# Result buffers of their own with whole-row transfers, and a tile of y moved behind the last products

## The chip, the cores and the metric

The kernel runs on one core of a Trainium2 chip. The metric is the device time of one execution in microseconds (us). The matrix engine is called TensorE (PE in the profile, PEld for its weight loads), the others are VectorE (DVE), ScalarE (ACT), GpSimd (POOL) and SyncE (SP). SP, ACT and POOL issue transfers.

## What is computed

The input x has 2048 rows of 512. With xn its layer norm without scale, the kernel computes a Fourier mixing s of xn and a gate g, and adds:

```python
xn  = layernorm(x)                                   # over the 512 columns
a   = xn @ dft_hid_re.T ;  b = xn @ dft_hid_im.T
s   = dft_seq_re @ a - dft_seq_im @ b                # 2048 x 512
h   = relu(xn @ w1 + b1)                             # 2048 x 1792
g   = silu((h * h) @ w2 + b2)                        # 2048 x 512
out = x + s * g
```

## The kernel before, in words

All products are float32 values split into a high and a low part (fp32r); each product takes three passes (high-high, high-low, low-high). Larger products go by a scheme of seven half-size products in place of eight (Strassen's), so their operands need sums of quarters (`sums_a`, `sums_b`), a rounding to the high part on ScalarE (L68) and a subtraction for the low part on VectorE (L71), and seven accumulators are joined at the end (`combine`: a copy on ScalarE, L260, then four steps on VectorE, L261 to L264).

**First stage.** The sequence transform is done first: for each block c of 256 columns of the transform (c = 0 to 7), over eight chunks j of 256 rows. Blocks 0 and 1 are done plainly, blocks 2 to 7 by the seven products. A chunk of the transform is loaded (`load_c`, L210), summed and split (`moving`) two chunks ahead; three raw loads are in flight. TensorE takes 42 matmuls a chunk (L321). Behind the last chunk the accumulators are combined and split into `pq`. The second factor, the hidden transform, is `stage2(c, t)`: 25 matmuls (L308) into one accumulator, a copy to the buffer `ysb` (L313) and a store of 128 rows of y (L315). The two tiles t = 0 and 1 of block c - 1 are done behind chunks 1 and 2 of block c. In this stage a scheduler sets the order on each engine, from the order in which the code is written.

In block 7 the next stage is prepared too: the rows of mean and scale (`load_rows`), two halves of the transposed input (`xt_half`: a load, two steps L346, sums, split), and the loads of the prepared first weights (`load_w1`, L501), which take the places of chunks of xn as TensorE is done with them.

**Last stage.** The order on each engine is written out by hand. First the hidden layer: 28 units, `hidden(n, c, p)`, for four blocks c of 512 rows and seven pairs p of hidden tiles (L572), each combined, squared and stored. Unit 0 comes first, then the two tiles of y of block 7, then the other units. Then the outer product: the same 28 units, `outer` (L620), whose operands are fetched, summed and split two units ahead (`operand`, L597, L228 to L230, L68, L71). After the seventh unit of a block the seven accumulators are combined into `e`, a buffer of four 128 x 512 results, C21, C11, C22 and C12, named z in the profile. There is one place for `e`; each block uses it again. `finish(*done, h)` runs behind the units p = 1 and p = 2 of the following block (p = 1 and 4 in the last): it takes silu on ScalarE (L656), multiplies by y (`fin`, L660) in place, and GpSimd adds the result into `out` in DRAM, where x was copied earlier (L650). The last block's results are handled in a tail of their own, in which x is loaded (`load_fin`) and added on VectorE.

Transfers on one engine's queue are issued in the order of the program; an instruction that waits holds up those behind it.

Of the kernel before, what the change touches and what calls it, by code (L numbers as in the profile page):

```python
# [10 lines left out]
ALU = mybir.AluOpType  # L11

P = 128
S, D, F = 2048, 512, 1792
NS, ND, NF = S // P, D // P, F // P
NJ, NP = NS // 2, NF // 2
# [45 lines left out]
def fnet_gated_kernel(ctx, tc, x, xt, ct, wd, w1, w2, b1, b2, out):  # L62
# [28 lines left out]
    def buf(tag, shape, name, dtype=F32, bufs=1):  # L91
        return pool.tile(shape, dtype, tag=tag, bufs=bufs, name=name)
# [539 lines left out]
    def load_fin(c):  # L632

        fin[c] = []
        for n, src in enumerate((Y[c], x[c * TC:(c + 1) * TC])[:1 + (c == NTC - 1)]):
            for m in range(2):
                tag = f"pq{n}{m}" if c < NTC - 1 else (("g0a", "sx"), ("g0b", "pq10"))[n][m]
                t = buf(tag, [P, 2, 512], f"fin{c}_{n}{m}")
                for i in range(2):
                    nc.sync.dma_start(t[:, i].rearrange("p (k e) -> p k e", k=2), at(src, 2 * m + i))  # L640
                fin[c].append(t)

    def finish(c, e, h):

        for k in (2, 0) if h == 0 else (1, 3):
            silu(e, k)
            times(c, e, k)
        for k in range(2):
            n = c * TC + (1 - h) * 256 + k * P
            nc.gpsimd.dma_start(out[n:n + P].rearrange("p (b e) -> p b e", b=2), e[:, h:4:2, k * 256:(k + 1) * 256],  # L650
                                accum_op=ALU.add)

    def silu(e, k, cols=slice(0, 2)):

# [3 lines left out]
    def times(c, e, k, cols=slice(0, 2)):  # L658
        w = slice(cols.start * 256, cols.stop * 256)
        nc.vector.tensor_tensor(e[:, k, w], e[:, k, w], fin[c][k // 2][:, k % 2, w], op=ALU.mult)  # L660
# [22 lines left out]
    for c, j in steps:  # L683
        if j == 0:
            ms = banks(c)
        g = part.pop((c, j))
        for p in ORDER:
            a, (grp, b) = PRODUCTS[p]
            mm(product(ms, p), XC[j][:, a], lambda b_: g[grp][:, b_, b], j == 0, j == NJ - 1)
        if c == PLAIN:  # L690
            if j == 4:
                nc.vector.transpose(stats_t, stats.rearrange("p m h j -> p (m h j)"))
                for q in range(4):
                    nc.sync.dma_start(rows[:, q * 32:(q + 1) * 32], stats_t[q * 32:(q + 1) * 32, :])
        if j in (1, 2):
            y_stored = stage2(c - 1, j - 1)
        if PLAIN <= c < PLAIN + NTC - 1 and j == 2:
            part_ = slice((c - PLAIN) * TC, (c - PLAIN + 1) * TC)
            with tc.issue_after(y_stored.ins):
                nc.sync.dma_start(out[part_], x[part_])  # L700
        if (c, j) in jobs:
            make_w(*jobs[c, j])
        if j == NJ - 1:
            e = buf("e", [P, 4, 512], f"c{c}")
            combine(e, ms)
            for m, dh, k in ((0, 0, C11), (1, 1, C22), (1, 0, C12), (0, 1, C21)):
                pq(c, m, dh, e[:, k])
        prep()
        if c == NC - 1:

            if j == 2:
                e = buf("e", [P, 8, 256], "rows0")
                load_rows(0, e[:, 0:4])
            if j in (2, 4):
                first = xt_half(0, j // 2 - 1, lambda k: e[:, 4:8] if (j, k) == (2, "r") else
                                turn_of(k, True))
                next(first)
            if j in (3, 6):
                list(first)
                kept.clear()  # L720
            if j > 3:
                load_w1(j - 4)

# [243 lines left out]
```

## Time and profile before

| | |
|---|---|
| median of 3 runs | 700.67 us (700.66 to 702.34) |
| the profiled execution | 700.18 us, span from first to last instruction 698.4 us |
| TensorE busy | 682.2 us, 98% of the span |
| VectorE / ScalarE / GpSimd busy | 578.7 / 346.0 / 15.6 us |
| granted TensorE clock, mean | 0.997 |

A line of a group or timeline names the source line, the engine, the operation and "written <- read". In square brackets or behind the bar stands the idle time of the engine before it and what ended that. In windows the five busy times are those of PE, PEld, DVE, ACT and POOL, followed by the granted clock, the DMA engines' share and GB/s. For transfers the last number is the time from issue to landing.

### The profile page before, as it was taken

How to read it: one execution, taken by the hardware profiler on the slowest of the kernel's cores; microseconds unless marked ns; L12 is line 12 of the kernel's file. 1: busy time of each engine (PE TensorE's matmuls, PEld its weight loads, DVE VectorE, ACT ScalarE, POOL GpSimd, SP SyncE). 2: the span in 40 equal slices, each digit the busy share in tenths (PEclk: the TensorE clock that was granted, in tenths of full speed). 3: DMA queues.
4: the chain of work that ended last, by engine and by line, in shares of the span. 5: the costliest groups of instructions: out<-in, count | busy, mean ns of one | idle time of the engine just before them, and what ended most of it. 6: DMA issues, size and time to landing. Idle time of an engine off the chain costs nothing.

```text
span 698.4 us, 12740 instructions
## 1 busy us (share of the span) xinstructions
PE 682.2 (98%) x5179; PEld 645.3 (92%) x5179; DVE 578.7 (83%) x866; ACT 346.0 (50%) x463; POOL 15.6 (2%) x20
## 2 busy tenths in 40 slices
PE   8999999999999999999999999999999999989797
PEld 5778889999999999999999989999999999979797
DVE  7998975589599698797798697989988799969696
ACT  3444644334353544544452326675867864435351
POOL 0000000000000000000000000000000100101011
PEclk9999999999999999999999999999999999999999
DMA  8622440733674763845835998284487954656655
GB/s 321 237 91 92 139 171 27 252 138 134 216 268 136 271 226 111 302 132 173 298 93 189 400 381 265 117 297 170 166 294 313 367 203 161 156 168 153 180 168 104
DMA packets 52250, 141.09 MB, mean 202 GB/s; under 512 B 4912, under 2 KB 18736, under 8 KB 50992
## 3 DMA queue, kind: packets, MB, share of 16 engines
q1 hardware_dynamic: 44896, 122.46, 50.2%
q10 hardware_dynamic: 3456, 12.58, 4.5%
q0 software_dynamic: 3840, 5.24, 4.2%
q8 instruction: 40, 0.66, 0.4%
q14 instruction: 18, 0.15, 0.1%
HBM read 97.00 MB, written 46.42 MB: 205 GB/s over the span
## 4 chain that ended last, share of the span: by engine, by line
PE 75%; DVE 14%; DMA 4%; issue 4%; ACT 2%; POOL 0%; DVEq 0%; ACTq 0%; POOLq 0%; SPq 0%
PE m_b L321 21%; PE yps L308 13%; PE hps L572 9%; PE pq_b L374 7%; PE hps_b L572 5%; DVE block L71 4%; PE m_bb L321 4%; PE m_ba L321 4%; PE m L620 3%; PE hps_ba L572 3%; DMA out<-z 2%; PE pq_ba L374 2%; DMA raws<-in_xt 1%; PE pq_bb L374 1%; PE hps_bb L572 1%
## 5 line engine op out<-in xcount | busy, mean ns | idle before, releaser
L321 PE MATMUL m_b<-g,block 128*128 128x256 f32 x1080 | 129.0, 276 | 0.0
L321 PEld LDWEIGHTS m_b<-g,block 128*128 128x128 f32 x1080 | 125.5, 188 | 0.1
L68 ACT ACTIVATE g<-raws 128x768 fp32r<-128x768 f32 (+2 forms) x65 | 57.4, 885 | 88.7 <-PE m_b L321 41.1
L71 DVE TENSOR_TENSOR g<-raws,g 128x768 fp32r<-128x768 f32 (+2 forms) x65 | 65.5, 1008 | 40.1 <-ACT g L68 40.0
L308 PE MATMUL yps<-wd,pq 128*128 128x512 f32 (+1 forms) x414 | 92.8, 374 | 0.0
L308 PEld LDWEIGHTS yps<-wd,pq 128*128 128x128 f32 x414 | 74.4, 188 | 13.7
L71 DVE TENSOR_TENSOR g<-sums,g 128x1024 fp32r<-128x1024 f32 x48 | 58.7, 1222 | 12.3 <-ACT g L68 12.3
L572 PE MATMUL hps<-xT,block 128*128 128x256 f32 x504 | 59.1, 276 | 0.0
L68 ACT ACTIVATE g<-sums 128x1024 fp32r<-128x1024 f32 x48 | 50.3, 1049 | 16.7 <-PE m_ba L321 7.8
L572 PEld LDWEIGHTS hps<-xT,block 128*128 128x128 f32 x504 | 58.0, 188 | 0.0
L374 PE MATMUL pq_b<-g,block 128*128 128x512 f32 x180 | 47.4, 394 | 0.5 <-DVE g L71 0.4
L321 PE MATMUL m_b<-g,xc 128*128 128x256 f32 x360 | 45.0, 276 | 0.0
L321 PEld LDWEIGHTS m_b<-g,xc 128*128 128x128 f32 x360 | 42.8, 188 | 0.1
L620 PE MATMUL m_b_o<-w,block 128*128 128x256 f32 x360 | 42.6, 276 | 0.0
L374 PEld LDWEIGHTS pq_b<-g,block 128*128 128x128 f32 x180 | 33.2, 188 | 9.6 <-DVE block L71 2.1
L620 PEld LDWEIGHTS m_b_o<-w,block 128*128 128x128 f32 x360 | 41.6, 188 | 0.0
L572 PE MATMUL hps_b<-xT,block 128*128 128x256 f32 x288 | 34.9, 276 | 0.3 <-DVE xT L71 0.3
L68 ACT ACTIVATE block<-hr 128x1792 fp32r<-128x1792 f32 (+1 forms) x15 | 23.8, 1587 | 21.8 <-PE m_bb_o L620 6.1
L222 DVE TENSOR_TENSOR sums<-raws 128x512 f32<-128x512 f32 x49 | 33.6, 686 | 1.0 <-DMA raws<-in_ct 0.7
L572 PEld LDWEIGHTS hps_b<-xT,block 128*128 128x128 f32 x288 | 33.6, 188 | 0.5 <-DVE xT L71 0.5
L583 ACT ACTIVATE raws<-raws,b1s 128x512 f32<-128x512 f32 x42 | 28.0, 716 | 12.2 <-DVE raws L263 12.0
L620 PE MATMUL m_b_o<-block 128*128 128x256 f32 x270 | 32.1, 276 | 0.0
(236 smaller groups left out, 1210.1 us busy)
## 6 DMA issues: line engine op xcount, KB each, us to landing
raws<-in_ct SPq DMA_DIRECT2D x63, 512.0 KB, 3.6
w1d<-w0g SPq DMA_DIRECT2D x21, 512.0 KB, 3.2
block<-w1d SPq DMA_DIRECT2D x6, 1792.0 KB, 10.4
hd<-raws ACTq DMA_DIRECT2D x18, 512.0 KB, 4.9
hr<-hd SPq DMA_DIRECT2D x15, 512.0 KB, 4.4
block<-w2d SPq DMA_DIRECT2D x3, 1792.0 KB, 14.2
y<-ysb SPq DMA_DIRECT2D x16, 256.0 KB, 3.3
fin<-y SPq DMA_DIRECT2D x16, 256.0 KB, 5.3
```

The lines of the kernel that those rows point to most:

```text
L68: nc.scalar.activation(hi, src, AF.Copy)
L71: return nc.vector.tensor_tensor(lo, src, hi.bitcast(F32), op=ALU.subtract)
L222: nc.vector.tensor_tensor(t[:, 0:2], r[:, 0:1].to_broadcast([P, 2, 256]), r[:, 1:3], op=ALU.add)
L308: nc.tensor.matmul(ps[:, s], PQ[c, m, k // 2][:, a_, w:w + P], WD[m, k][:, b_, s], start=n == 0, stop=n > len(todo) - 3, skip_group_check= ...
L321: nc.tensor.matmul(ps[:, d * CW:(d + 1) * CW], w[:, a_, d * P:(d + 1) * P], mv(b_), start=first and d == 0 and (a_, b_) == (HI, HI), stop= ...
L374: nc.tensor.matmul(accs[c][k], w, g[:, b_, 2 * h:2 * h + 2], start=j == 0 and h == 0 and (a_, b_) == (HI, HI), stop=j == NJ - 1 and h == 1 ...
L572: nc.tensor.matmul(product(ms, k), W1[p][a][:, a_, q * P:(q + 1) * P], xT[c, q][:, b_, b], start=share not in first, stop=q == 1 and (a_, ...
L583: nc.scalar.activation(x_[:, s], x_[:, s], AF.Relu, bias=b1s[:, f:f + 1])
L620: nc.tensor.matmul(m[:, k * 256:(k + 1) * 256], g[:, a_, a, k * P:(k + 1) * P], W2[p][b][:, b_], start=p == 0 and k == 0 and (a_, b_) == ( ...
```

## The change

```diff
@@ load_fin
-                tag = f"pq{n}{m}" if c < NTC - 1 else (("g0a", "sx"), ("g0b", "pq10"))[n][m]
+                tag = f"pq{n}{m}" if c < NTC - 1 else (("g0a", "sx"), ("g0b", "xc0"))[n][m]
@@ finish
-        for k in (2, 0) if h == 0 else (1, 3):
+        z = buf(f"pq1{h}", [P, 2, 2, 256], f"z{c}_{h}")
+        for b, k in enumerate((C11, C12) if h == 0 else (C21, C22)):
             silu(e, k)
-            times(c, e, k)
-        for k in range(2):
-            n = c * TC + (1 - h) * 256 + k * P
-            nc.gpsimd.dma_start(out[n:n + P].rearrange("p (b e) -> p b e", b=2), e[:, h:4:2, k * 256:(k + 1) * 256],
-                                accum_op=ALU.add)
+            nc.vector.tensor_tensor(z[:, :, b], e[:, k].rearrange("p (k e) -> p k e", k=2),
+                                    fin[c][k // 2][:, k % 2].rearrange("p (k e) -> p k e", k=2), op=ALU.mult)
+        n = c * TC + h * 256
+        nc.gpsimd.dma_start(out[n:n + 256].rearrange("(k p) e -> p k e", k=2), z.rearrange("p k b e -> p k (b e)"),
+                            accum_op=ALU.add)
@@ the chunks of the first stage
-        if j in (1, 2):
-            y_stored = stage2(c - 1, j - 1)
+        if j in ((1, NJ - 1) if c == NC - 1 else (1, 2)):
+            y_stored = stage2(c - 1, int(j > 1))
@@ the same, in block 7
+            if j in (3, 5):
+                list(first)
+                kept.clear()
             if j == 2:
                 e = buf("e", [P, 8, 256], "rows0")
                 load_rows(0, e[:, 0:4])
-            if j in (2, 4):
-                first = xt_half(0, j // 2 - 1, lambda k: e[:, 4:8] if (j, k) == (2, "r") else
+            if j in (2, 3):
+                first = xt_half(0, j - 2, lambda k: e[:, 4:8] if (j, k) == (2, "r") else
                                 turn_of(k, True))
                 next(first)
-            if j in (3, 6):
-                list(first)
-                kept.clear()
```

In `finish` the product with y is written to one of two buffers, z0 and z1 (places pq10 and pq11), as 256 whole rows of 512; each half of a block goes out in one transfer of 512 KB with rows of 2 KB, where it went in two of 256 KB with pieces of 1 KB. The two upper quarters come first, then the two lower. Since pq10 is taken, the last block's second half of x lands in xc0, the place of the first pair of second weights.

In block 7 the second tile of y of block 6 is made behind chunk 7 and no longer behind chunk 2. The second half of the transposed input is requested behind chunk 3 (before: 4) and worked on behind chunk 5 (before: 6).

The scheduler makes of this the following. On TensorE in block 7 (`m_...` are the accumulators of the block, `g_7_j` the split chunk j, `yps_1` the tile of y that moves, `hps` the first unit of the next stage), before:

```order
L321 MATMUL m_ba_3648<-g_7_2_3694,block 128x256 x6
L308 MATMUL yps_1_3827<-wd_676,pq_0_0_3624 128x512 x6
L308 MATMUL yps_1_3827<-wd_676,pq_0_1_3633 128x512 x6
L308 MATMUL yps_1_3827<-wd_753,pq_1_0_3630 128x512 x6
L308 MATMUL yps_1_3827<-wd_753,pq_1_1_3627 128x512 x5
L308 MATMUL yps_1_3827<-wd_753,pq_1_1_3627 128x256 x2
L321 MATMUL m_bb_3649<-g_7_3_3776,block 128x256 x6
```

The tile stands between chunks 2 and 3. In the change its first seven matmuls stand within chunk 6,

```order
L321 MATMUL m_b_7_3646<-g_7_6_3948,block 128x256 x6
L321 MATMUL m_b_7_3646<-g_7_6_3949,block 128x256
L321 MATMUL m_b_7_3647<-g_7_6_3949,block 128x256
L321 MATMUL m_ba_3648<-g_7_6_3949,block 128x256
L308 MATMUL yps_1_4105<-wd_676,pq_0_0_3624 128x512 x6
L308 MATMUL yps_1_4105<-wd_676,pq_0_1_3633 128x512
L321 MATMUL m_bb_3649<-g_7_7_4000,block 128x256
L321 MATMUL m_b_7_3646<-g_7_6_3949,block 128x256 x5
```

and the other 18 between the last product of chunk 7 and the first unit of the hidden layer:

```order
L321 MATMUL m_ba_3648<-g_7_7_4001,block 128x256 x6
L308 MATMUL yps_1_4105<-wd_676,pq_0_1_3633 128x512 x5
L308 MATMUL yps_1_4105<-wd_753,pq_1_0_3630 128x512 x6
L308 MATMUL yps_1_4105<-wd_753,pq_1_1_3627 128x512 x5
L308 MATMUL yps_1_4105<-wd_753,pq_1_1_3627 128x256 x2
L572 MATMUL hps_bb<-xT_0_3900,block 128x256 x3
```

So the products of chunks 3 to 7 move forward by the tile, and the tile moves back to the stage's end. On SP's queue in the same block (`raws<-in_ct` the last load of the transform, `block<-w1d` prepared weights, `y_69<-ysb` stores of y):

```order
 L210 DMA raws<-in_ct 128x1024
 L315 DMA y_69<-ysb_3772 128x512
+L501 DMA block<-w1d_903 128x3584
 L210 DMA raws<-in_ct 128x1024
-L501 DMA block<-w1d_903 128x3584
-L315 DMA y_69<-ysb_3772 128x512
 L501 DMA block<-w1d_904 128x3584
 L340 DMA raws<-in_xt 128x1024
```

```order
 L506 DMA w1a_4209<-w1d_909 128x2x768
 L507 DMA w1b_4210<-w1d_909 128x2x1024
+L315 DMA y_69<-ysb_3772 128x512
 L315 DMA y_69<-ysb_4254 128x512 x2
 L333 DMA rows_4295<-rows 128x256 x4
```

The first weight passes the load of chunk 7, and the second store of y goes behind all seven weights, right ahead of the two stores of the next block. On ScalarE at the end of the second block of 512 rows in the last stage (`z_6618` is the buffer of the combination, `m_..._o` the accumulators), with the semaphores that each instruction waits for, before:

```order
L68 ACTIVATE block<-raws 128x1792 [waits DVE_49,DMAHW1_49,PE_49,Activation_49]
L260 ACTIVATE z_6618<-m_bc_o_6260 128x512 [waits DMASW6_49,DMASW5_49,DMASW7_49,DMASW4_49,PE_49]
L613 ACTIVATE m_ba_o_6628<-b2s 128x512
L613 ACTIVATE m_b_o_6629<-b2s 128x512 [waits DVE_49]
L613 ACTIVATE m_b_o_6630<-b2s 128x512 [waits DVE_49,PE_49]
```

and in the change:

```order
L68 ACTIVATE block<-raws 128x1792 [waits DVE_49,DMAHW1_49,PE_49,Activation_49]
L260 ACTIVATE z_6618<-m_bc_o_6260 128x512 [waits PE_49]
L613 ACTIVATE m_ba_o_6628<-b2s 128x512
L613 ACTIVATE m_b_o_6629<-b2s 128x512 [waits DVE_49]
L613 ACTIVATE m_b_o_6630<-b2s 128x512 [waits DVE_49,PE_49]
```

The order is the same; the four waits for GpSimd's transfers (DMASW) are gone from L260. GpSimd's queue holds six transfers from z where it held twelve.

## Prediction

> **What bounds the kernel now.** I read the page's engine shares first, then who TensorE waited for over the whole span, then the windows and the timeline at those waits.
>
> ```profile
> PE 682.2 (98%) x5179; PEld 645.3 (92%) x5179; DVE 578.7 (83%) x866; ACT 346.0 (50%) x463; POOL 15.6 (2%) x20
> PE m L620 <- DVE z L261: 3.5, 1, 3.5
> PE m_bc_o L620 <- ACT z L260: 3.4, 1, 3.4
> PE hps_ba L572 <- DVE c L264: 1.1, 1, 1.1
> PE hps_b L572 <- DVE xT L71: 0.3, 1, 0.3
> ```
>
> TensorE is busy for 98% of 698.4 us, so only its own gaps and its own speed are worth anything. The list of its waits is short. Two long ones stand in the last stage and two short ones at its entry; what else is listed (3.3 us) belongs to the first microseconds. Where the two long ones come from is seen in the timeline.
>
> ```profile
> 612.73 1.72 ACT L68 ACTIVATE block<-raws 128x1792 fp32r<-128x1792 f32 x1 [3.05 <-PE m_bb_o L620]
> 614.15 1.07 POOL L650 DMA_DIRECT2D out<-z  x1 [5.22 <-issue]
> 614.48 2.02 DVE L71 TENSOR_TENSOR block<-raws,block 128x1792 fp32r<-128x1792 f32 x1 [1.17 <-ACT block L68]
> 620.24 0.60 ACT L260 ACTIVATE z<-m_bc_o 128x512 f32<-128x512 f32 x1 [5.79 <-DMA out<-z]
> 620.87 1.22 DVE L261 TENSOR_TENSOR z<-m_b_o,z 128x1024 f32<-128x1024 f32 x1 [4.36 <-ACT z L260]
> 620.89 0.96 PE L620 MATMUL m_bc_o<-w,block 128*128 128x256 f32 x6 [3.37 <-ACT z L260]
> 658.13 1.23 DVE L261 TENSOR_TENSOR z<-m_b_o,z 128x1024 f32<-128x1024 f32 x1 [4.62 <-ACT z L260]
> 659.41 4.61 PE L620 MATMUL m<-w,block 128*128 128x256 f32 x24 [3.52 <-DVE z L261]
> out<-z POOLq DMA_DIRECT2D x1, 256.0 KB, 6.0
> ```
>
> A block's four results sit in one buffer, and the next block's first copy into it (L260) may not run before all four accumulating transfers out of it have landed. The fourth was issued at 614.15 and took 6.0 us (last row, the transfers of that moment): 620.15, and L260 starts at 620.24. VectorE's combination follows, and TensorE stands for 3.37 us because its next products write the accumulator that L260 reads. 37 us later it is the same: 3.52 us. This is a chain transfer, ScalarE, VectorE, TensorE, with VectorE itself idle for 4.36 and 4.62 us.
>
> The second stall has a price behind it, which the windows show (busy time of PE, PEld, DVE, ACT, POOL, then the granted clock).
>
> ```profile
> 621.00:624.00 3.00, 3.00 (x27) 3.00 (x28) 2.86 (x3) 0.93 (x2) 0.00 (x0) 1.00 0.00 0
> 661.40:662.40 1.00, 1.00 (x6) 1.00 (x6) 0.90 (x2) 0.37 (x1) 0.00 (x0) 0.50 0.00 0
> 584.00:617.50 33.50, 33.50 (x296) 33.32 (x294) 30.56 (x36) 15.07 (x13) 4.39 (x4) 1.00 0.68 186
> 663.86 0.40 PE L620 MATMUL m_bc_last<-w,block 128*128 128x256 f32 x2
> ```
>
> After the first stall the clock stays at 1.00. After the second it is 0.50 at 661.4. A matmul of this size takes 33.50 / 296 = 0.113 us in the busy stretch 584 to 617.5; the 24 that started at 659.41 gave way to the next (last row) only at 663.86, so they held TensorE 4.45 us, where 24 x 0.113 = 2.72 are due. The first matmul behind any wait shows about 0.11 us of its own start, so I charge the slow clock with 1.6 us. [...] This trace agrees with a halving after 3.52 us idle and none after 3.37. [...]
>
> **The change part by part.** *Results (finish).* The product with y now goes into z buffers of its own, in the places pq10 and pq11. L260 then waits for VectorE's four multiplies, not for the transfers; these are done well before the transfer of 614.15, which needs them, so the wait is gone. What is late next? In the first of the two blocks L260 can run behind the split that ScalarE has from 612.73 to 614.45, and VectorE's L261 behind its split, at 614.48 + 2.02 = 616.5. Its three large steps at 1.25 us end at 620.2. TensorE reaches the new block at 617.5: its 24 first products need two accumulators that are free by 615.7, the next groups start at 617.5 + 2.7 = 620.2 and 622.9, and the biases in front of them are one copy of 0.6 us each behind L261 and L263, at 618.4 and 620.8. So there is no new wait: 3.37 us off. In the transition from the first block to the second L260 had no transfer to wait for, and the first product of the new block is this row:
>
> ```profile
> 584.00 0.84 PE L620 MATMUL m_bc_o<-w,block 128*128 128x256 f32 x6
> ```
>
> It carries no wait: TensorE passed without a gap, with the same combination on VectorE beside it. In the last block the margins are thinner. VectorE was idle there from 658.13 - 4.62 = 653.5 and TensorE from 659.41 - 3.52 = 655.9. Less 3.37, L261 runs from 650.1 to 651.4 and TensorE comes at 652.5; L263 ends at 653.9, the two biases behind it at 655.0, and the first product that needs them, 27 products on, starts at 655.6. I take 3.52 off, and since TensorE no longer stands, the 1.6 us of the slow clock too; bounds for this place are 3.0 (a few tenths of new wait) and 5.1.
>
> The multiplies write two pieces of 256 where they wrote 512 in one.
>
> ```profile
> L660 DVE TENSOR_TENSOR z<-z,fin 128x512 f32<-128x512 f32 x15 | 9.8, 685 | 0.7 <-ACT z L656 0.7
> L262 DVE TENSOR_TENSOR raws<-hps_b,raws 128x512 f32<-128x512 f32 x14 | 9.7, 692 | 2.2 <-PE hps_b L572 0.9
> 680.41 1.29 DVE L660 TENSOR_TENSOR z<-z,fin 128x512 f32<-128x512 f32 x2
> ```
>
> L262 is an operation of the same size that writes two pieces: 692 against 685 ns. Twelve of them cost 0.1 us on VectorE, which had 33.50 - 30.56 = 2.9 us to spare in the block above; I take 0 and bound it by 0 and 0.1. Twelve accumulating transfers become six of twice the size. Nothing but the kernel's end and the same z buffer a block (33 us) later waits for them. A transfer of 256 KB took 6.0 us above, so a double one is bounded by 6 and 12; the third block's last multiplies end at 681.7 (last row), about 672 with what is saved before them, and their transfer lands by 684, before the end. Taken: 0. The operand x of the last block now lands in xc0, which a weight holds until TensorE's second step of that block; the queue issues that load last and nothing stands behind it but the final stores: 0.
>
> *The tile of y behind the last products (entry of the last stage).*
>
> ```profile
> 374.71 5.62 PE L308 MATMUL yps<-wd,pq 128*128 128x512 f32 x25
> 377.39 1.22 DVE L71 TENSOR_TENSOR g<-sums,g 128x1024 fp32r<-128x1024 f32 x1
> 408.52 0.69 DVE L264 TENSOR_TENSOR c<-m_ba,c 128x512 f32<-128x512 f32 x1
> ```
>
> These 25 matmuls hold TensorE for 5.4 us (374.7 to about 380.1) in the middle of block 7; the chunks' products then run 5.4 us earlier, and 18 of the 25 (16 whole ones and two halves) now stand between the last product and the first matmul of the next stage: 17 x 0.225 = 3.8 us. VectorE's combination of block 7 starts with the last products, so relative to TensorE it is done 3.8 us sooner (L264, its last step, ended at 409.2 with TensorE waiting), and the waits of 0.28 and 1.11 us are covered: 1.39 off, bounds 0 and 1.39. Cover that is taken away: at 374.7 the y tile let VectorE finish chunk 4's splits (the last at 378.6); the products of chunk 4 now start at 374.6 + 42 x 0.113 = 379.4 and want the last of them at 380.7, so that holds.
>
> Two steps pass others in SP's queue. First, the load of chunk 7 now stands behind the weight load that waits for chunk 3's first product.
>
> ```profile
> 377.50 0.33 SPq L210 DMA_DIRECT2D raws<-in_ct  x1
> 380.60 0.33 SPq L501 DMA_DIRECT2D block<-w1d  x1
> 385.37 0.32 SPq L501 DMA_DIRECT2D block<-w1d  x1
> 386.38 0.33 SPq L340 DMA_DIRECT2D raws<-in_xt  x1
> block<-w1d SPq DMA_DIRECT2D x1, 1792.0 KB, 8.2
> block<-w1d SPq DMA_DIRECT2D x1, 1792.0 KB, 9.8
> raws<-in_xt SPq DMA_DIRECT2D x1, 512.0 KB, 10.0
> ```
>
> The weight is issued 5.4 us earlier, at 375.2, and takes 8.2 to 9.8 us: 383.4 to 385.0. A 512 KB load behind the second such weight landed at 386.38 + 10.0 = 396.4, 1.2 us after it (385.37 + 9.8 = 395.2). So chunk 7 lands at 384.6 to 386.2 instead of soon after its own issue at 377.5. VectorE now has a sum of chunk 7 ahead of chunk 6's splits: from that landing to the first product that wants chunk 6's sums lie a sum step, a split of 768 columns, four small steps and ScalarE's rounding.
>
> ```profile
> L222 DVE TENSOR_TENSOR sums<-raws 128x512 f32<-128x512 f32 x49 | 33.6, 686 | 1.0 <-DMA raws<-in_ct 0.7
> L68 ACT ACTIVATE g<-sums 128x1024 fp32r<-128x1024 f32 x48 | 50.3, 1049 | 16.7 <-PE m_ba L321 7.8
> 375.64 0.96 DVE L71 TENSOR_TENSOR xT<-rows,xT 128x768 fp32r<-128x768 f32 x1 [0.58 <-ACT xT L68]
> 372.84 0.42 DVE L224 TENSOR_TENSOR sums<-sums,raws 128x256 f32<-128x256 f32 x1
> ```
>
> That is 0.69 + 0.96 + 4 x 0.42 + 1.05 = 4.4 us, and the product comes at 374.6 + 3 x 4.75 + 1.36 = 390.2. The last harmless landing is 385.8: cost 0, at most 0.4, and 7 matmuls of y stand in the middle of chunk 6 as a further cushion.
>
> Second, the store of this y half is now queued behind all weights, and ScalarE's next copy into the same buffer waits until it has landed.
>
> ```profile
> 406.14 0.74 SPq L507 DMA_DIRECT2D w1b<-w1d  x1
> w1b<-w1d SPq DMA_DIRECT2D x1, 1024.0 KB, 17.3
> 416.42 0.60 ACT L313 ACTIVATE ysb<-yps 128x512 f32<-128x512 f32 x1 [6.30 <-PE yps L308]
> 421.74 4.92 PE L572 MATMUL hps<-xT,block 128*128 128x256 f32 x42
> ```
>
> The last weight landed at 406.14 + 17.3 = 423.4. All the loads are released 4 to 5.4 us earlier, so it should land near 418.5 and the small store just behind it, near 419. The copy, due at about 415, then ends at 419.7, and TensorE wants its bank at 421.7 - 1.4 = 420.3. Cost 0, with 0.6 us to spare; if the weights came no earlier, the copy would end near 424.8 and TensorE would stand 4.5 us.
>
> **The sum.** 3.37 + 3.52 + 1.6 + 1.39 = 9.9 us. The profiled execution took 700.18 us (span 698.4 and 1.8 around it): 690.3. The median of the runs is 700.67, 0.5 more: I forecast **690.8 us**.
>
> **The rivals.** *The entry gives nothing:* chunk 7 late or the bank of y held takes back 1.4 us. For it speaks the thin 0.6 us, against it that all loads move up together. 700.67 - 8.5 = 692.2; if the whole 4.5 us came, 695.3. *The clock term is absent* from the timed runs: 700.67 - 8.3 = 692.4. For it speaks that only one of two near-equal gaps was punished; against it that the timed median lies above the profiled run that has the drop. [...] *VectorE gives it back:* with the stalls gone it has 30.6 of 33.5 us to do, and if L261 of the last block came 1 to 3 us late the gain there would shrink to give 693 to 695. The first transition without a gap speaks against it. *Slower than before:* the split writes on VectorE are much dearer than 0.69 us. Four a block fill the 2.9 us to spare at 1.4 us each; from there each further us costs 4 us a block, and over two and a half blocks 9.9 + 2.1 us are gone at about 2.6 us each: 703 or more. L262 at 692 ns speaks against it. *It does not do what it says:* some other use of pq10 or pq11 holds the multiplies back and L260 with them; time near 700.
>
> **How the numbers follow.** Forecast 0.60; entry gives nothing 0.14; no clock term 0.11; VectorE gives back 0.08; slower 0.04; without effect 0.03. The range 689.9 to 693.8 takes in the forecast with its unknowns (0.9 below for further small waits that vanish) and the first two rivals. A difference under 0.3%, 2.1 us, can't be told from none: faster 0.93, same 0.03, slower 0.04.
>
> **What would show it.** Right: TensorE's waits on L260 and L261 are gone from its list, and those at L572 too; the granted clock is 1.00 from 584 to the tail; six transfers from z; L260 names no transfer. Wrong: a wait of TensorE at the copy of y near 420, or at chunk 6 near 390; a multiply longer than 0.7 us; a granted clock under 1.00 inside the last stage. A time over 694 would refute the sum.

## The result and the profile after

The changed kernel takes 689.87 us (median of 6 runs, 689.39 to 690.28). The kernel before, run again beside it, takes 701.13 us (700.23 to 703.87). The ratio is 0.9833, with a 95% interval of 0.9815 to 0.9851: faster, as forecast, by 11.3 us where 9.9 were forecast. The time lies 0.03 us below the low end of the range, less than the executions differ among themselves.

The engine shares of the changed kernel's page and the whole list of TensorE's waits:

```profile
PE 680.2 (99%) x5179; PEld 643.8 (94%) x5179; DVE 577.8 (84%) x866; ACT 345.9 (50%) x463; POOL 9.8 (1%) x14
PE pq_b L374 <- ACT xc L68: 1.5, 3, 0.7
PE warm L396 <- DVE zeros L394: 1.2, 1, 1.2
PE hps L572 <- DVE h L264: 0.4, 1, 0.4
PE pq_b L374 <- DVE g L71: 0.4, 1, 0.4
```

The two waits of 3.4 and 3.5 us on L260 and L261 are gone, and so are those of 1.1 and 0.3 us at the entry of the last stage. One wait is new: 0.4 us at L572 on VectorE's L264. The timeline of the changed kernel, at the first product of the second, third and fourth block of results and what stands around it:

```profile
583.26 0.84 PE L620 MATMUL m_bc_o<-w,block 128*128 128x256 f32 x6
...
613.61 0.58 ACT L260 ACTIVATE z<-m_bc_o 128x512 f32<-128x512 f32 x1
615.68 1.22 DVE L261 TENSOR_TENSOR z<-m_b_o,z 128x1024 f32<-128x1024 f32 x1
616.62 0.84 PE L620 MATMUL m_bc_o<-w,block 128*128 128x256 f32 x6
...
647.48 0.58 ACT L260 ACTIVATE z<-m_bc_o 128x512 f32<-128x512 f32 x1
649.03 1.22 DVE L261 TENSOR_TENSOR z<-m_b_o,z 128x1024 f32<-128x1024 f32 x1
651.34 2.88 PE L620 MATMUL m<-w,block 128*128 128x256 f32 x24
...
654.05 0.50 PE L620 MATMUL m_bc_last<-w,block 128*128 128x256 f32 x3
```

None of these rows has idle time or a releaser behind it. L260 ran 6.6 us earlier than before (613.61 against 620.24), ahead of VectorE, and TensorE went through both places without a gap. The same 24 matmuls that held TensorE for 4.45 us before (659.41 to 663.86) now take 2.71 (651.34 to 654.05). The window from the middle of the first stage to the tail shows the clock (after the five busy times):

```profile
374.00:673.00 299.00, 298.42 (x2554) 295.20 (x2554) 264.47 (x350) 173.85 (x211) 8.60 (x10) 1.00 0.68 236
```

The same rows in both profiles split the gain of the two profiled executions (700.18 and 690.28, 9.90 us apart):

| row (TensorE) | before | after | gain so far | this part |
|---|---|---|---|---|
| first product of the second block | 584.00 | 583.26 | 0.74 | entry and hidden layer 0.74 |
| first product that waited, third block | 620.89 | 616.62 | 4.27 | first stall 3.53 |
| first product that waited, fourth block | 659.41 | 651.34 | 8.07 | second stall 3.80 |
| next product, 24 on | 663.86 | 654.05 | 9.81 | slow clock 1.74 |
| whole execution | 700.18 | 690.28 | 9.90 | rest 0.09 |

At the entry the timeline of the changed kernel shows two small waits that the list of before doesn't have (the last number of the last row, a transfer, is from issue to landing):

```profile
404.20 0.87 PE L572 MATMUL hps_bb<-xT,block 128*128 128x256 f32 x6
405.02 16.25 SPq L315 DMA_DIRECT2D y<-ysb  x3
419.77 1.16 ACT L313 ACTIVATE ysb<-yps 128x512 f32<-128x512 f32 x2 [13.98 <-DMA y<-ysb]
420.42 1.66 PEld L572 LDWEIGHTS hps<-xT,block 128*128 128x128 f32 x14 [0.44 <-ACT ysb L313]
468.82 2.48 DVE L346 TENSOR_TENSOR xr<-xr,rows 128x1024 f32<-128x1024 f32 x2 [2.40 <-DMA xr<-in_xt]
478.91 0.77 PEld L572 LDWEIGHTS hps<-xT,w1a 128*128 128x128 f32 x6 [0.62 <-PE hps L572]
...
y<-ysb SPq DMA_DIRECT2D x1, 256.0 KB, 14.6
```

The store of the moved tile was issued at 405.02 and landed 14.6 us later, at 419.6. ScalarE's copy waited for it, and the weight loads of TensorE for the copy, 0.44 us. At 468.8 VectorE waited for a load of transposed input, and TensorE stood for it near 479. Whether the moved tile brings both is seen in the experiments: the first wait yes, the second no.

Transfers and multiplies of the changed kernel, by line (duration in ns, least, median, most; then from issue to landing in us):

```profile
L648 DVE TENSOR_TENSOR z<-z,fin x12: 683/684/687, 596.2 to 671.7; 128x512 f32<-128x512 f32 x12
L651 POOL DMA_DIRECT2D out<-z x6: 1190/1196/1245, 597.8 to 672.8; - x6
DMA to landing us min/median/max: 5.9/6.5/8.3
```

The multiplies with split writes cost what they cost before (684 ns at the median, 685 before). The accumulating transfers of 512 KB took 5.9 to 8.3 us, where the 12 of 256 KB took 4.1 to 6.5 in the kernel before.

### The profile page after: what moved, and what is told of

The parts are those of the page before. It is cut to its first block, busy times and chain, and to the rows that moved or that the text cites. A ratio compares the mean times of both kernels' runs of the same rounds, so it can differ in the third digit from the quotient of the medians.

```text
span 688.5 us, 12730 instructions
## 1 busy us (share of the span) xinstructions
PE 680.2 (99%) x5179; PEld 643.8 (94%) x5179; DVE 577.8 (84%) x866; ACT 345.9 (50%) x463; POOL 9.8 (1%) x14
## 4 chain that ended last, share of the span: by engine, by line
PE 88%; DVE 6%; DMA 4%; issue 1%; ACT 0%; DVEq 0%; ACTq 0%
PE m_b L321 23%; PE yps L308 11%; PE m_b_o L620 10%; PE hps L572 8%; PE pq_b L374 7%; PE m_bb L321 5%; PE m_ba L321 5%; PE hps_b L572 4%; PE m L620 3%; DMA y<-ysb 2%; PE hps_ba L572 2%; PE pq_ba L374 2%; PE m_ba_o L620 1%; PE m_bb_o L620 1%; PE m_bc_o L620 1%; DMA xr<-in_xt 1%
## 5 line engine op out<-in xcount | busy, mean ns | idle before, releaser
L572 PE MATMUL hps<-xT,block 128*128 128x256 f32 x504 | 59.2, 277 | 0.1
L572 PEld LDWEIGHTS hps<-xT,block 128*128 128x128 f32 x504 | 58.0, 188 | 0.4 <-ACT ysb L313 0.4
L620 PE MATMUL m_b_o<-w,block 128*128 128x256 f32 x360 | 42.6, 276 | 0.0
L620 PEld LDWEIGHTS m_b_o<-w,block 128*128 128x128 f32 x360 | 41.6, 188 | 0.0
L572 PE MATMUL hps_b<-xT,block 128*128 128x256 f32 x288 | 34.7, 277 | 0.0
L583 ACT ACTIVATE raws<-raws,b1s 128x512 f32<-128x512 f32 x42 | 28.1, 716 | 12.9 <-DVE raws L263 12.8
L572 PEld LDWEIGHTS hps_b<-xT,block 128*128 128x128 f32 x288 | 33.6, 188 | 0.0
L620 PE MATMUL m_b_o<-block 128*128 128x256 f32 x270 | 32.1, 276 | 0.0
```

The source lines that it names most:

```text
L572: nc.tensor.matmul(product(ms, k), W1[p][a][:, a_, q * P:(q + 1) * P], xT[c, q][:, b_, b], start=share not in first, stop=q == 1 and (a_, ...
L583: nc.scalar.activation(x_[:, s], x_[:, s], AF.Relu, bias=b1s[:, f:f + 1])
L620: nc.tensor.matmul(m[:, k * 256:(k + 1) * 256], g[:, a_, a, k * P:(k + 1) * P], W2[p][b][:, b_], start=p == 0 and k == 0 and (a_, b_) == ( ...
```

## The experiments

Two theories stood at the start on why the timed gain (11.3 us) exceeds the profiled one (9.9). A: the profile of before is typical, and the difference lies elsewhere. B: TensorE's clock halves behind either stall in a varying number of executions, and the profiled one was a quick one. The first four kernels ran in one group, with the kernel before at 701.57 us (23 executions).

**before_again.** The kernel before, unchanged, for more executions and a second profile.

> The kernel before, unchanged, to see how its own executions spread. Theory A (the profiled execution speaks for all): each has one slow-clock stretch behind the second stall, 700.2 to 700.9 us, mean clock 0.997 in all. Theory B (the clock falls behind a stall in some executions and not in others, and behind either of the two): times lie between about 699 and 704 us in steps of 1.6 to 2 us, and the longer the time the lower the mean clock (1.000 without, 0.997 with one, 0.994 or so with two). If the longer runs show the same clock as the shorter, B falls.

Measured: 702.86 us (700.71 to 704.96, 12 executions), ratio 1.0007 (0.9989 to 1.0025). Its profiled execution took 703.38 us. TensorE's waits there, the two rows that waited, and two windows right behind them:

```profile
PE m L620 <- DVE z L261: 4.2, 1, 4.2
PE m_bc_o L620 <- ACT z L260: 3.5, 1, 3.5
620.50 0.97 PE L620 MATMUL m_bc_o<-w,block 128*128 128x256 f32 x6 [3.50 <-ACT z L260]
661.99 4.62 PE L620 MATMUL m<-w,block 128*128 128x256 f32 x24 [4.22 <-DVE z L261]
```

```profile
622.00:624.00 2.00, 2.00 (x12) 2.00 (x11) 1.97 (x2) 0.34 (x1) 0.00 (x0) 0.50 0.00 0
664.00:666.00 2.00, 2.00 (x11) 2.00 (x11) 1.86 (x4) 1.35 (x3) 0.00 (x0) 0.50 0.00 0
```

The clock is 0.50 behind both stalls, where the first profile had 1.00 behind the first. All executions of the kernel before in the three groups of these experiments, by mean granted clock:

```
clock        0.997-0.998  0.996   0.995   0.994   0.992-0.993  0.990   0.989
executions   6            6       11      11      10           11      2
median us    700.1        700.9   701.6   701.9   703.0        703.5   705.0
```

None of 57 had a clock of 0.999 or more; the kernels without stalls below have 0.998 to 1.000. So all but the one at 0.998 had at least one drop, and the profiled execution of before, at 0.997, is among the quickest tenth or so. Theory A falls. Of theory B the steps in the times are not seen, nor an execution at 1.000; the longer time at the lower clock is.

**results_only.** The changed kernel without the moved tile (its loop over chunks as before).

```diff
-        if j in ((1, NJ - 1) if c == NC - 1 else (1, 2)):
-            y_stored = stage2(c - 1, int(j > 1))
+        if j in (1, 2):
+            y_stored = stage2(c - 1, j - 1)
...
-            if j in (2, 3):
+            if j in (2, 4):
```

> Only the results' part (own z buffers, whole-row transfers, x half in xc0); the tile of y stays behind chunk 2. The waits at L260 are gone, the waits of 0.28 and 1.11 us at the entry of the last stage stay. Theory A: 701.1 - 7.4 - 1.6 = 692.1. Theory B (the median of the kernel before holds more than one slow stretch): the changed kernel's 689.9 plus the 0.7 us that the entry gained in its profile, 690.6, and a clock of 1.000 in every run.

Measured: 690.06 us (688.97 to 691.61, 6 executions), ratio 0.9835 (0.9811 to 0.9858), clock 0.999 to 1.000. The part on results alone gives the whole gain. The wait at the entry, for which the tile was moved, is in TensorE's list of this kernel, but small:

```profile
PE hps_ba L572 <- DVE c L264: 0.2, 1, 0.2
```

It was 1.1 and 0.9 us in the two profiles of before, where up to this place the code is the same. So the 1.39 us of the prediction were one execution's reading of a wait that varies.

**tile_only.** The kernel before with the moved tile and its loads, results in place.

```diff
-        if j in (1, 2):
-            y_stored = stage2(c - 1, j - 1)
+        if j in ((1, NJ - 1) if c == NC - 1 else (1, 2)):
+            y_stored = stage2(c - 1, int(j > 1))
...
```

> Only the tile of y behind chunk 7; results go out of the one buffer as before. The two stalls at L260 and the spread of the kernel before stay. The entry's gain as predicted is 1.4 us (699.7), as the changed kernel's profile shows it 0.7 us (700.4): a new wait of 0.44 us for the copy of y near 420 and one of 0.45 us near 479 should be seen in the profile.

Measured: 702.63 us (700.09 to 706.72, 12 executions), ratio 1.0015 (0.9994 to 1.0035). The tile alone gives nothing that can be measured; neither 699.7 nor 700.4 came. In its profile the waits of before at the entry are gone, of the two new ones only that for the copy is seen (0.3 us by the weight loads), and both stalls are there, longer:

```profile
PE m L620 <- DVE z L261: 5.3, 1, 5.3
PE m_bc_o L620 <- ACT z L260: 3.7, 1, 3.7
```

**own_two_transfers.** The changed kernel, but each half of a block goes out in two transfers of 256 KB by columns, pieces of 1 KB as before.

```diff
-        nc.gpsimd.dma_start(out[n:n + 256].rearrange("(k p) e -> p k e", k=2), z.rearrange("p k b e -> p k (b e)"),
-                            accum_op=ALU.add)
+        for b in range(2):
+            nc.gpsimd.dma_start(out[n:n + 256, b * 256:(b + 1) * 256].rearrange("(k p) e -> p k e", k=2), z[:, :, b],
+                                accum_op=ALU.add)
```

> The changed kernel, but each half of a block goes out in two transfers of 256 KB with pieces of 1 KB again, out of the z buffers. If the buffers do the work: 689.9 within 0.4 us, no wait at L260. Rival: the whole rows and fewer transfers matter too (shorter transfers, less beside the loads): 0.5 to 2 us slower than the changed kernel.

Measured: 689.96 us (689.68 to 692.27, 5 executions), ratio 0.9839 (0.9815 to 0.9863). With the buffers there, whole rows and fewer transfers bring nothing that can be measured.

The next four ran beside the kernel before at 702.48 us (11 executions). In **first_only** and **second_only** the own buffers serve one block of results, the other blocks go out in place as before; the tile is moved in both. The edit of first_only; second_only has (1,) in place of (0,):

```diff
+        if c in (0,):
+            z = buf(f"pq1{h}", [P, 2, 2, 256], f"z{c}_{h}")
...
+        else:
+            for k in (2, 0) if h == 0 else (1, 3):
+                silu(e, k)
+                times(c, e, k)
...
```

> The whole change, but the results buffers of their own are used in the first block of results alone; the other blocks go out in place as before. So the first stall of TensorE is taken away and the second stays. Theory B (both stalls cost their own length and, in a varying number of executions, a halved clock behind them; each is worth its own part): from the 701.6 of the kernel before, off 3.6 for the stall and 0 to 1.7 for the clock behind it: 696.3 to 698.0, granted clock 0.995 to 0.997, a second stall of 3.7 to 5.5 us with the clock at 0.50 behind it. The rival (the transfers of the next block just come later against a TensorE that is earlier, so the second stall grows by what the first gave): 700 to 701.6, a second stall of 7 us or more.

> The whole change, but the results buffers of their own are used in the second block of results alone: the first stall stays, the second goes. Theory B (each stall is worth its length and its clock): off 3.7 to 4.4 for the second stall and 1.6 to 2 for the clock behind it, 701.6 - 5.3 to 6.4: 695.2 to 696.3; the clock behind the first stall is halved in some executions and not in others, so the times spread over some 2 us, mean clock 0.996 to 1.000. The prediction's terms taken from one execution (3.52 and 1.6 for the second stall, and never a halved clock behind the first): 696.5 with a clock of 1.000 in every execution.

Measured: first_only 697.10 us (695.90 to 697.30, 6 executions), ratio 0.9917 (0.9900 to 0.9935), clock 0.995 to 0.998. second_only 696.32 us (695.01 to 697.15, 6 executions), ratio 0.9910 (0.9890 to 0.9930), clock 0.994 to 1.000. Of TensorE's waits, the stall that is left and one at L572, first_only ahead:

```profile
PE m L620 <- DVE z L261: 3.7, 1, 3.7
...
PE hps L572 <- ACT ysb L313: 1.1, 1, 1.1
```

```profile
PE m_bc_o L620 <- ACT z L260: 3.6, 1, 3.6
PE hps L572 <- ACT ysb L313: 1.6, 1, 1.6
```

The stall that was left did not grow by what the other gave, so the rival falls. The two stalls are worth 5.4 and 6.2 us, together 11.5: about the whole gain of 11.3 (both kernels have the moved tile as well). In second_only the two executions with a clock of 0.999 and 1.000 took 695.01 and 695.12 us, the four with 0.994 to 0.997 took 695.85 to 697.15. So the clock seems to drop behind the first stall in most executions, at a cost of some 0.7 to 2.1 us, in which other waits that vary are contained. The prediction's reading of one profile, no drop behind the first stall, does not hold for before_again and tile_only, whose clock is 0.50 there; in the profile of second_only, the execution of 695.01 us, it is 1.00.

The wait for ScalarE's copy of y, of which the prediction had said 0 with 0.6 us to spare, is here 1.1 and 1.6 us. **ysb_own** takes this wait away: the tiles of block 7 are copied into a place of the first stage that is free by then.

```diff
-            ysb[c] = buf("sx", [P, 2, D], f"ysb{c}")
+            ysb[c] = buf("sx" if c < NC - 1 else "g0a", [P, 2, D], f"ysb{c}")
```

> The whole change, and the two tiles of y of block 7 are copied into a buffer of their own (a free place of the first stage), so that ScalarE's copy near 420 no longer waits for the store of the moved tile. If the 0.44 us that TensorE waits there in the changed kernel are time: 689.4. If they are taken back by the next thing that is late (VectorE held by the load of transposed input until 468.8, for which TensorE waits 0.45 near 479): the wait near 420 is gone, that near 479 grows by about as much, and the time stays at 689.9 with 0.3 to either side.

Measured: 689.53 us (689.41 to 689.88, 4 executions), ratio 0.9813 (0.9793 to 0.9834). The copy no longer waits for a transfer, and the wait near 479 is 0.37 us, not longer than the 0.45 in the changed kernel:

```profile
420.32 0.60 ACT L313 ACTIVATE ysb<-yps 128x512 f32<-128x512 f32 x1 [4.86 <-PE yps L308]
478.46 0.94 PE L572 MATMUL hps<-xT,w1a 128*128 128x256 f32 x6 [0.37 <-DVE h L264]
```

So the later wait did not take it back in this execution; whether it is time is looked at again below.

**eight_transfers.** Up to here it was taken as given that the four transfers of a block land late. This kernel is the one before, with one edit: each transfer of 256 KB cut into two by columns.

```diff
-            nc.gpsimd.dma_start(out[n:n + P].rearrange("p (b e) -> p b e", b=2), e[:, h:4:2, k * 256:(k + 1) * 256],
-                                accum_op=ALU.add)
+            for b in range(2):
+                nc.gpsimd.dma_start(out[n:n + P, b * 256:(b + 1) * 256], e[:, h + 2 * b, k * 256:(k + 1) * 256],
+                                    accum_op=ALU.add)
```

> The kernel before, with each of its four accumulating transfers of 256 KB a block cut into two of 128 KB by columns: eight a block, the same bytes. If the stalls are set by a chain of transfers that follow one another on GpSimd's queue, each issued when the one before has landed, both grow: with 4.2 us for 256 KB and 6.5 for 512 KB I estimate 3.0 for 128 KB by a straight line, 0.3 between them, so eight take 26 us where four take 21.5, and the last ones more: 5 to 10 us longer at each of two stalls, 711 to 722 us, and L260 ends its wait on a transfer 5 to 10 us later. If the bytes or something else than the chain sets the landing of the last one, the stalls and the time stay as before: 701.6.

Measured: 690.75 us (690.35 to 691.20, 4 executions), ratio 0.9830 (0.9809 to 0.9851), clock 1.000. Both expectations were wrong, and the first by its sign: without any buffer of its own and without the moved tile the kernel gains as much as by the whole change, within what the runs can tell. GpSimd's issues in the kernel before, with the landing of the first:

```profile
598.63 1.14 POOL L650 DMA_DIRECT2D out<-z  x1 [41.26 <-DVE z L660]
603.18 1.09 POOL L650 DMA_DIRECT2D out<-z  x1 [3.40 <-issue]
...
out<-z POOLq DMA_DIRECT2D x1, 256.0 KB, 4.2
```

and in eight_transfers, with ScalarE's first copy of the next block:

```profile
598.60 2.68 POOL L651 DMA_DIRECT2D out<-z  x3 [41.21 <-DVE z L661]
602.03 0.84 POOL L651 DMA_DIRECT2D out<-z  x1 [0.76 <-issue]
...
610.90 0.85 POOL L651 DMA_DIRECT2D out<-z  x1 [2.86 <-issue]
616.33 0.60 ACT L260 ACTIVATE z<-m_bc_o 128x512 f32<-128x512 f32 x1 [1.85 <-DMA out<-z]
...
out<-z POOLq DMA_DIRECT2D x1, 128.0 KB, 3.1
```

Before, the second transfer is issued 0.35 us after the first has landed (598.63 + 4.2 = 602.83), and the third and fourth 0.36 and 0.31 us after the one ahead of them (603.18 + 4.3 = 607.48, 607.84 + 6.0 = 613.84). The profile names no releaser for these issues; that they wait for a landing is read from the times. Cut in two, three go out one behind the other, and only the fourth waits for a landing (598.60 + 3.1 = 601.7, issued at 602.03). The last of the block is issued at 610.90 and not 614.15, and L260 runs at 616.33, 3.9 us earlier and in time for TensorE. These times fit a limit on what GpSimd's queue holds at once, in packets or in bytes.

The last four ran beside the kernel before at 702.18 us (11 executions). **row_transfers** is the changed kernel with each transfer cut into two of 128 whole rows, 256 KB in 128 pieces.

```diff
-        n = c * TC + h * 256
-        nc.gpsimd.dma_start(out[n:n + 256].rearrange("(k p) e -> p k e", k=2), z.rearrange("p k b e -> p k (b e)"),
-                            accum_op=ALU.add)
+        for k in range(2):
+            n = c * TC + h * 256 + k * P
+            nc.gpsimd.dma_start(out[n:n + P], z[:, k].rearrange("p b e -> p (b e)"), accum_op=ALU.add)
```

> The changed kernel with each transfer of 256 rows cut into two of 128 whole rows: four of 256 KB a block, each 128 pieces of 2 KB. If GpSimd's queue holds a limited number of pieces (a transfer of 128 pieces counts 144 packets, three of them went out 0.9 us apart; one of 256 counts 272, and a second never went out before the first had landed): both halves are issued as soon as their multiply is done, some 1.2 us apart, though they carry 512 KB together. If bytes are what is limited (three of 128 KB were in flight together, two of 256 KB never): the second is issued 0.3 us after the first has landed, 4 to 5 us later. The time is the same by both, 689.9 with 0.5 to either side, since nothing waits for these transfers.

Measured: both halves go out within 1.8 us, and the first takes 4.2 us to land, so 512 KB are in flight together. GpSimd's first issues in row_transfers:

```profile
598.78 1.79 POOL L652 DMA_DIRECT2D out<-z  x2 [41.12 <-DVE z L648]
603.52 1.73 POOL L652 DMA_DIRECT2D out<-z  x2 [2.95 <-DVE z L648]
```

So it is not bytes, nor a number of transfers, since three went out together in eight_transfers and never two before. The packets of GpSimd's queue, in the order before, eight_transfers, row_transfers (packets, MB, share of 16 engines):

```profile
q0 software_dynamic: 3840, 5.24, 4.2%
```

```profile
q0 software_dynamic: 4032, 5.24, 4.4%
```

```profile
q0 software_dynamic: 2304, 5.24, 4.0%
```

Where this queue carries nothing else, the 12 transfers of before hold 3264 packets (from 580 us to the end), 272 each (256 pieces and 16 more), and 8 of eight_transfers 1152 (597 to 625 us), 144 each (128 and 16). So the three totals above are 12 x 272, 24 x 144 and 12 x 144, and each time 576 of other transfers are left. Three of 144 (432) were in flight together, a fourth (576) was not, and two of 272 (544) never were. A limit on packets somewhere between 432 and 543 is an estimate from these counts that fits every row; no run measured the limit itself. The one execution took 691.43 us, 1.0 us over the upper end of what was expected. Its profile shows the late load of transposed input again, with a longer wait:

```profile
469.85 2.48 DVE L346 TENSOR_TENSOR xr<-xr,rows 128x1024 f32<-128x1024 f32 x2 [3.62 <-DMA xr<-in_xt]
...
479.96 0.94 PE L572 MATMUL hps<-xT,w1a 128*128 128x256 f32 x6 [1.13 <-DVE h L264]
```

**after_again** (the changed kernel) and **ysb_again** (the kernel of ysb_own), side by side:

> The changed kernel as it is, beside the other three of this group. Both theories: 689.9 (689.4 to 690.4), clock 0.999 to 1.000. If the wait for ScalarE's copy of y near 420 differs from execution to execution with the landing of the weights ahead of the store (0.4 us in one execution of the changed kernel, 1.1 and 1.6 in those of first_only and second_only), the times spread by up to 1 us; if it is always the 0.4, by 0.3.

> The kernel of ysb_own, beside the changed kernel. If the copy's wait near 420 costs time in typical executions: 0.3 to 0.8 us below the changed kernel in the same group; if VectorE's later wait for the load of transposed input takes it back: the same within 0.3.

Measured: after_again 690.61 us (689.55 to 691.29, 6 executions), ratio 0.9835 (0.9806 to 0.9863). ysb_again 689.70 us (689.36 to 690.24, 5 executions), ratio 0.9826 (0.9798 to 0.9854). The changed kernel spreads over 1.7 us, with a clock of 0.998 in three executions, and the wait for the copy is in its profile with 0.8 us:

```profile
PE hps L572 <- ACT ysb L313: 0.8, 1, 0.8
```

Without that wait the median is 0.9 us lower here, and over all executions 689.53 (9, none over 690.24) against 690.00 (12, up to 691.29). The ranges overlap and so do the intervals: a gain of about half a microsecond is likely, not settled.

**eight_and_tile.** The edit of eight_transfers and that of tile_only together.

```diff
+        if j in ((1, NJ - 1) if c == NC - 1 else (1, 2)):
+            y_stored = stage2(c - 1, int(j > 1))
...
+            for b in range(2):
+                nc.gpsimd.dma_start(out[n:n + P, b * 256:(b + 1) * 256], e[:, h + 2 * b, k * 256:(k + 1) * 256],
+                                    accum_op=ALU.add)
```

> The kernel of eight_transfers (results in place, eight transfers of 128 KB a block) with the moved tile of y and its loads, so without the results buffers. If buffers are not needed once the transfers no longer wait for one another: as the changed kernel, 689.9, and 0.9 less than the 690.75 of eight_transfers, whose first unit still waited 1.1 us for the combination of block 7. If the moved tile gives nothing measurable, as it did with the stalls still there: 690.75. If the place of the results decides after all: 692 or more, with a wait of TensorE at L260 or L261.

Measured: 691.33 us (689.63 to 693.25, 6 executions), ratio 0.9849 (0.9820 to 0.9878), clock 0.999 to 1.000. TensorE's matmuls have no wait at L260, L261 or the entry in its profile. Yet it isn't quicker than eight_transfers, and it spreads over 3.6 us. So the moved tile gave nothing measurable with the stalls there (tile_only) or without them (results_only against the changed kernel, eight_and_tile against eight_transfers). What makes this kernel spread is open.

**One row in all profiles.** The first product of the second block of results (L620, at 584.00 in the kernel before) cuts each profiled execution in two. Ahead of it these kernels differ only in the place of the tile, of the loads moved with it and of its copy; the stalls come behind it.

| profiled execution | start of the row, us | from there to the end, us |
|---|---|---|
| before; before_again | 584.00; 583.48 | 116.18; 119.90 |
| tile_only | 584.93 | 119.91 |
| first_only (second stall left) | 583.59 | 113.51 |
| second_only (first stall left) | 584.18 | 110.83 |
| results_only; eight_transfers | 582.60; 584.02 | 107.07; 107.00 |
| changed kernel; after_again | 583.26; 584.21 | 107.02; 107.00 |
| own_two_transfers; row_transfers; eight_and_tile | 583.65; 584.29; 584.00 | 107.14; 107.14; 106.99 |
| ysb_own; ysb_again | 582.77; 583.23 | 107.11; 107.01 |

Without stalls all nine executions need 107.0 to 107.1 us behind the row. So the stalls with their clock cost 9.1 us in the quick profile of before and 12.8 in two others, the second alone 6.5 and the first alone, with no drop, 3.8. Ahead of the row the tile gives nothing: the row starts at 582.60 to 584.02 in the four executions with the tile in its old place, at 583.26 to 584.93 in the eight with the tile moved, and at 582.77 and 583.23 with a copy buffer of its own. The 0.74 us of the table above lie within this spread. And TensorE's wait near 479 is not brought by the tile: eight_transfers, with the tile in its old place, has it too, with 0.39 us.

## Why the prediction was right, and where it was wrong

**The sum** was 9.9 us from the profiled execution of before, and the profiled executions are 9.90 apart. That is luck of errors that cancel, as the table shows: the stalls gave 3.53 and 3.80 where 3.37 and 3.52 were taken, the clock 1.74 where 1.6, the entry 0.74 where 1.39, and those 0.74 us are the spread of the executions and no gain of the tile. By the medians the stalls and their clock are the whole gain of 11.3 us, where 8.5 were taken, and the entry gives nothing that can be measured, where 1.39 were.

**The stalls: the mechanism was right, the size was a little small.** The chain transfer, ScalarE, VectorE, TensorE is gone, and nothing took its place. By TensorE's weight loads the stalls were 0.2 us longer than by its matmuls (3.5 and 3.4); the list of waits of the kernel before:

```profile
PEld m L620 <- DVE z L261: 3.7, 1, 3.7
PEld m_bc_o L620 <- ACT z L260: 3.6, 1, 3.6
```

What the prediction didn't ask is why the fourth transfer was issued as late as 614.15. It took the issue for given and found a cure in more room. eight_transfers shows a second one: by the times of issue and landing above, one transfer of 256 pieces was in flight at a time, and three of 128.

**The step that failed** is the last one of the sum: "The median of the runs is 700.67, 0.5 more: I forecast 690.8 us". It carried what the median of before has over its profiled execution into the changed kernel. That surplus consists of longer stalls and of clock drops behind both (before_again, second_only), and the change removes it with them. The term put at nothing under it is the slow clock behind the first stall, which one profile had not shown. In before_again the two rows of the stalls lie 661.99 - 620.50 = 41.49 us apart, where the changed kernel needs 34.72; of the 6.8 us between, 4.4 are the second stall by the weight loads and the rest, about 2.4, the slow clock behind the first. Without the surplus the forecast would have been 690.3, as the profiled execution of the changed kernel. The range fell short at the low end for the same reason: it left 0.9 us for small waits that vanish and nothing for the stalls being worth more in a typical execution (5.4 and 6.2 us each with its clock, where the prediction had 3.4 and 5.1) than in the quick one that was profiled. That the median fell just outside the range and not just inside is chance: the changed kernel's second median, 690.61, lies within it.

**The entry was mis-sized.** 1.39 us were one execution's waits (0.92 in before_again, 0.2 in results_only), and a cost taken as 0 came: the copy that waits for the store of y (0.44 by the weight loads, 0.8, 1.1 and 1.6 us in four profiles). The prediction had named it, given it 0.6 us to spare, and sized the landing right, 419 against 419.6, but in one execution only. The load of transposed input near 469, which it had not named, holds TensorE up in some executions with the tile in either place. Chunk 7's load behind a weight cost nothing, as said: no wait of TensorE stands between 375 and 392.

**The clock term.** The rival without a clock term in the timed runs (the 9.9 us less 1.6, so 8.3) was wrong the other way round: the drop comes more often than in the profile. In second_only, whose one gap was 3.8 us by the weight loads of its profile, four of six executions had a clock under 0.998, and so had 56 of 57 of the kernel before. The length of the gap alone doesn't tell whether the drop comes: by TensorE's matmuls 3.50 us were followed by 0.50 in before_again, and 3.6 us by 1.00 in second_only:

```profile
622.00:624.00 2.00, 2.00 (x20) 2.00 (x20) 1.86 (x3) 0.60 (x1) 0.00 (x0) 1.00 0.00 0
```

So the 3.52 us with a drop and the 3.37 without, in the one profile that the prediction read, are no limit between the two. How long the gaps of the executions without a profile were is not known. The runs agree that it is not every execution.

**Zero-cost terms.** Split writes: 684 ns against 685, right. Double transfers: 5.9 to 8.3 us, within the bounds of 6 and 12 but for a tenth. VectorE did not give the gain back, and nothing of the slower rival showed.

## What to carry to other kernels

A buffer that waits for its stores can be cured at the store: look at whether transfers of one queue are issued one by one, each just after the last has landed, and at how many pieces each has, before spending memory on a second buffer. When a cost varies between executions, a difference taken from one profile belongs to that execution: don't carry the distance between profile and median over to a kernel in which its cause is gone. A wait of about a microsecond that one profile shows, and that hangs on a load's landing, is not yet a microsecond of gain.

## What the runs showed of the hardware that was not expected

On GpSimd's queue three transfers of 144 packets (128 KB each, eight_transfers) or two of 144 (256 KB each, row_transfers) were in flight together, but never two of 272 (256 KB each, before), so packets fit and bytes do not. Gaps of 3.6 to 5.5 us on TensorE (by the weight loads, eight of them in five profiles) cost, with a clock of 0.50 to 0.52 behind six of the eight, 5.4 to 6.2 us each in the median. With them the times of before spread from 698.8 to 705.4 us; the 12 executions of the changed kernel lie between 689.4 and 691.3.

In some stretches TensorE makes some 2 to 4% fewer matmuls (87 or 88 in 10 us where others have 90 or 91) at a full share of busy time and a granted clock of 1.00. The same 10 us in tile_only and results_only, in this order (the number behind the first busy time counts matmuls):

```profile
440.00:450.00 10.00, 10.00 (x88) 10.00 (x87) 8.82 (x14) 5.67 (x9) 0.00 (x0) 1.00 0.26 105
```

```profile
440.00:450.00 10.00, 10.00 (x90) 10.00 (x89) 9.23 (x16) 6.19 (x9) 0.00 (x0) 1.00 0.28 112
```

In tile_only it lasts from 430 to 450 and from 480 to 520, in eight_and_tile (87 in this window) from 430 to 450, in before_again (87 and 88) from 630 to 640 and from 670 to 680. The matmuls are slower, none are missing: a group of 42 gives way to the next after 4.95 us in tile_only (430.31 to 435.26) and after 4.76 in results_only (429.83 to 434.59). It may be part of why tile_only and eight_and_tile gain nothing from the tile; its cause was not looked for and stays open.
